# Lightning attention into a PReLU MLP: the opening's list laid out anew from finer statements

## The chip, the cores and the metric

The kernel runs on one core of one Trainium2 chip. The metric is device time in microseconds, from the first to the last instruction of an execution. The kernel before takes 214.34 us, the median of three runs (214.21 to 216.0).

## The reference

Two layers in a row. The first is a causal linear attention with decay ("lightning attention"): 4 batches, 8 heads, 768 positions, head size 64, in blocks of 64 positions with a running 64x64 state per head. The second is an MLP with a learned slope for negative values: 3072 tokens of 512 features to 2048 and back to 512.

```
for b in range(nb):                       # blocks of 64 positions
    intra = einsum('bhic,bhjc->bhij', qb, kb) * Dmask          # Dmask[i,j] = lam**(i-j), i >= j
    intra = einsum('bhij,bhjd->bhid', intra, vb)
    inter = einsum('bhid,bhde->bhie', qb * lam**(pos+1), kv_state)
    out[:, :, sl] = intra + inter
    kv_state = lam**block * kv_state + einsum('bhsd,bhse->bhde', kb * lam**(block-1-pos), vb)
h = x @ w_in                              # x: the attention's output, [3072, 512]
g = maximum(h, 0) + alpha * minimum(h, 0)
return g @ w_out
```

Inputs and output are float32; the kernel computes in float16 with float32 accumulation.

## The kernel before, in words

**Work.** The kernel takes blocks of 128 positions. The tokens are cut into six chunks c of 512 (256 positions of two batches). Chunks 0 and 1 are the first 256 positions of all four batches, chunks 2 and 3 the next, 4 and 5 the last. A chunk has four *units* (chunk, one of two batches, one of two groups of four heads), numbered 0 to 23; a unit covers two blocks. Units of chunks 0 and 1 have no state to read in their first block.

**A unit's steps.** `load` brings q, k or v of one batch (512 KB; 256 KB for one head group) on SP's DMA queue. `cast` makes float16 copies; `key_decayed` makes kdec, the keys times their decay. `transposes` (or `transposed`, q or k alone) turns q and k on TensorE through PSUM, with a copy to qkT; with engine "D" SP does it by a DMA. `decayed` makes qdT, the queries times their decay. `cluster(old, new)` then interleaves two units on TensorE: the carried part of the old unit (qdT against the states RD), the scores of the new one, the old one's output from its masked scores, and the new one's keys against values (the new state's increment). Behind these it records the mask products of the new unit (`sm`, two on VectorE), the copy of the old unit's output into the chunk's xT, and the new unit's state updates (R, by ScalarE and VectorE, and RD). So all of a cluster's statements stand in one piece in each engine's queue.

**A chunk's MLP.** `up(c, f)` is one of 16 tiles of hidden features: four 128x512 matmuls against w_in, then ScalarE makes m = relu(-h) and VectorE g = m*(1-alpha)+h (`slope_product`; with `later` it is recorded further down). `down(c, t, part, 4)` is a quarter of an output tile of 128 tokens, four matmuls against one quarter of w_out. So a chunk has 16 up-projections and 16 down parts of four matmuls each. `store` copies the result to SBUF and sends it.

**PSUM.** Eight banks: "acc" (two banks, one buffer, for a cluster's output and key-value products), s0 and s1 (scores), "op", "tk" and two buffers of "h" (up-projections, down tiles, transposes, fills). `fill` issues matmuls whose result nobody reads, to keep TensorE running.

**Order.** Nothing is scheduled by a compiler: each engine's queue holds its instructions in the order in which the statements are called. The program has three parts: a prefix (constants, decay tables), a long list of calls written out (L595 to L905: units 0 to 18, chunk 0's and 1's MLP and chunk 2's up-projections), and a loop over chunks 3 to 5 that weaves `up(c)`, `down(c-1)` and the steps of the next units. The list is what the change replaces.

**Weights.** w_in and w_out come in quarters of 512 hidden features (1 MB of float32 each, converted to float16 by the DMA, 512 KB as written), issued by GpSimd (`load_win`, `load_wout`), whose queue is in order: an issue waits for the casts and products listed ahead of it. `gate(i, which)` is a tiny DMA on SP's queue that reads one element of a quarter; since SP's queue is in order too, no later load is issued until that quarter has landed. In the list of before, SP meets `gate(1, "in")` right behind the load of q of (1,0).

```
    for gi in range(NHP):                      # up: w_in quarter f // 4
        nc.tensor.matmul(h_ps, lhsT=w_in_sb[:, gi, ts(f, 128)], rhs=x, start=(gi == 0), stop=(gi == 3))
    for f in range(part * n, part * n + n):    # down: w_out quarter `part`
        nc.tensor.matmul(o_ps, lhsT=lhs(c, f, t), rhs=w_out_sb[:, f, :], start=(f == 0), stop=(f == NF - 1))
```

Of the kernel before, what the change touches and what calls it, by code (L numbers as in the profile page):

```python
# [11 lines left out]
def kernel(  # L12
# [16 lines left out]
    nc = tc.nc  # L29
# [7 lines left out]
    B, H, S, D = q.shape  # L37
    assert (B, H, S, D) == (4, 8, 768, 64)
    L = 128
    W = 2 * L  # L40
    NC = (S // W) * 2
# [28 lines left out]
        for n in range(1, S // L)  # L70
# [24 lines left out]
    def load_win(i):  # L95
        nc.gpsimd.dma_start(  # L96
            out=w_in_sb[:, :, ts(i, 512)],
            in_=moe_w_in[:, ts(i, 512)].rearrange("(g p) f -> p g f", p=128),
        )

    def load_wout(i):
        nc.gpsimd.dma_start(
            out=w_out_sb[:, ts(i, 4), :],
            in_=moe_w_out[ts(i, 512), :].rearrange("(f p) d -> p f d", p=128),
        )
# [73 lines left out]
    )  # L179
    rev_f = const.tile([128, 2], fp32, name="rev_f")  # L180
# [29 lines left out]
    def decay_mask(hp):  # L210
        nc.scalar.activation(dmask[:, :, hp], dmask[:, :, hp], AF.Exp)

# [29 lines left out]
    T = {}  # L242
# [107 lines left out]
    def cluster(old, new, eng="A", state_first=False, own=False):  # L350

        acc = ps.tile([128, 2, 512], fp32, tag="acc", name="acc")
        ot = [acc[:, a, 0:256].rearrange("p (h i) -> p h i", h=2) for a in range(2)]
        kv = [acc[:, a, 256:384].rearrange("p (h d) -> p h d", h=2) for a in range(2)]
        if own:
            kv = [bank_of("h", "kv")[:, 0:128].rearrange("p (h d) -> p h d", h=2) for a in range(2)]
        if old is not None:
            co, bo, ho = units[old]  # L360
            pbo, bb = co // 2, 2 * (co % 2) + bo
            to = T[old]
            for a in range(2):
                if 2 * pbo + a == 0:
                    continue
                for hp in range(2):
                    nc.tensor.matmul(  # L367
                        ot[a][:, hp, :].rearrange("p (e j) -> p e j", e=2),
                        lhsT=RD[bb, ho][:, a, hp].rearrange("p h d -> p (h d)"),
                        rhs=to["qdT"][:, :, hp, ds(a * 64, 64)],  # L370
                        start=(hp == 0),
                        stop=False,
                        skip_group_check=True,
                    )
        if new is not None:
            c, bi, hh = units[new]
            pb, b = c // 2, 2 * (c % 2) + bi
            t = T[new]
            s = [ps.tile([128, 2, 2, L], fp32, tag=f"s{hl}", name=f"s{hl}") for hl in range(2)]
            for hp in range(2):  # L380
                for e in range(2):
                    for a, hl in QUADS:
                        p = ds(hl * 64, 64)
                        nc.tensor.matmul(  # L384
                            s[hl][ds(a * 64, 64), hp, 1 - e, :].rearrange("p (e j) -> p e j", e=2),
                            lhsT=t["qkT"][p, 1, e, hp, ds(a * 64, 64)],
                            rhs=t["qkT"][p, 0, :, hp, ds(a * 64, 64)],
                            start=True,
                            stop=True,
                        )  # L390
        if old is not None:
            for hp in range(2):
                for e in range(2):
                    for hl, a in QUADS:
                        p = ds(a * 64, 64)
                        nc.tensor.matmul(  # L396
                            ot[a][ds(hl * 64, 64), hp, :],
# [39 lines left out]
        def state():  # L437
# [18 lines left out]
            for a in range(2):  # L456
                if pb == 0:
                    continue
# [489 lines left out]
```

## Time and profile before

| what | value |
|---|---|
| median of three runs | 214.34 us |
| profiled execution, span | 215.6 us |
| TensorE busy | 206.4 us (96%) |
| VectorE, ScalarE, GpSimd busy | 131.6, 116.7, 86.8 us |
| DMA packets | 33.90 MB, mean 157 GB/s |
| read from HBM, written | 27.27 MB, 6.29 MB |

The profile is of one execution, and the times in it are counted from that execution's first instruction. A row of a timeline gives start, length, engine, source line, operation, what is written and read, shapes, count and, in brackets, how long the engine had sat idle and what ended that. A row of a group gives count, then busy time and the mean length of one instruction in ns, then idle time ahead of them and its cause. A chain row gives start, length and what the chain of waits passes through. Matmuls are pipelined, so the length of one is longer than the distance to the next. Line numbers are those of the kernel before.

### The profile page before, as it was taken

How to read it: one execution, taken by the hardware profiler on the slowest of the kernel's cores; microseconds unless marked ns; L12 is line 12 of the kernel's file. 1: busy time of each engine (PE TensorE's matmuls, PEld its weight loads, DVE VectorE, ACT ScalarE, POOL GpSimd, SP SyncE). 2: the span in 40 equal slices, each digit the busy share in tenths (PEclk: the TensorE clock that was granted, in tenths of full speed). 3: DMA queues.
4: the chain of work that ended last, by engine and by line, in shares of the span. 5: the costliest groups of instructions: out<-in, count | busy, mean ns of one | idle time of the engine just before them, and what ended most of it. 6: DMA issues, size and time to landing. Idle time of an engine off the chain costs nothing.

```text
span 215.6 us, 5212 instructions
## 1 busy us (share of the span) xinstructions
PE 206.4 (96%) x2089; PEld 107.3 (50%) x2089; DVE 131.6 (61%) x254; ACT 116.7 (54%) x220; POOL 86.8 (40%) x160
## 2 busy tenths in 40 slices
PE   7998997889999999999999999999999999999993
PEld 7564443445444545455554554554545444444453
DVE  7894887664298969879876645745646344444000
ACT  6996787335776544657855545544434534444121
POOL 7285254503592745577677366357311000000000
PEclk9999999999999999999999999999999999999999
DMA  5999999999999999699549997043011011110212
GB/s 164 295 270 206 244 237 249 160 248 281 240 284 144 294 237 271 161 255 173 71 128 227 249 238 203 13 100 97 2 52 49 14 38 49 50 49 3 97 49 97
DMA packets 62478, 33.90 MB, mean 157 GB/s; under 512 B 18150, under 2 KB 59510, under 8 KB 62454
## 3 DMA queue, kind: packets, MB, share of 16 engines
q1 hardware_dynamic: 58182, 29.37, 56.6%
q0 software_dynamic: 4224, 4.19, 12.1%
q8 instruction: 16, 0.26, 0.5%
q14 instruction: 8, 0.07, 0.1%
q10 hardware_dynamic: 48, 0.01, 0.0%
HBM read 27.27 MB, written 6.29 MB: 156 GB/s over the span
## 4 chain that ended last, share of the span: by engine, by line
PE 72%; DMA 20%; SPq 3%; POOL 2%; ACT 1%; issue 1%; DVE 0%; ACTq 0%
PE o_ps L518 30%; PE h_ps L479 29%; PE o_ps L547 6%; DMA vraw<-in_v_dram 5%; DMA kraw<-in_k_dram 5%; DMA w_in_sb<-in_moe_w_in_dram 5%; DMA w_out_sb<-in_moe_w_out_dram 5%; PE s L384 2%; PE acc L396 2%; SPq L87 2%; PE acc L367 2%; PE acc L411 1%; POOL qk L252 1%; ACT o_sb L531 0%; POOL w_in_sb L96 0%
## 5 line engine op out<-in xcount | busy, mean ns | idle before, releaser
L503 DVE SCALAR_TENSOR_TENSOR g<-m,oma,h_ps 128x512 f16<-128x512 f32 x96 | 70.5, 745 | 55.7 <-ACT m L487 54.2
L479 PE MATMUL h_ps<-xT,w_in_sb 128*128 128x512 f16 x384 | 93.4, 379 | 0.6 <-DMA w_in_sb<-in_moe_w_in_dram 0.4
L487 ACT ACTIVATE m<-h_ps 128x512 f32<-128x512 f32 x96 | 56.9, 597 | 50.6 <-PE h_ps L479 49.0
L518 PE MATMUL o_ps<-w_out_sb,g 128*128 128x512 f16 x320 | 79.5, 379 | 2.3 <-DMA w_out_sb<-in_moe_w_out_dram 2.3
L479 PEld LDWEIGHTS <-w_in_sb 128*128 128x128 f16 x384 | 36.5, 98 | 43.5 <-DMA w_in_sb<-in_moe_w_in_dram 0.6
L518 PEld LDWEIGHTS <-g 128*128 128x128 f16 x320 | 30.3, 98 | 38.1 <-DMA w_out_sb<-in_moe_w_out_dram 1.8
L461 POOL COPY RD<-R 64x128 f16<-64x128 f16 x64 | 19.6, 306 | 41.0 <-DVE R L447 39.3
L422 DVE TENSOR_TENSOR sm<-s,dmask 128x512 f16<-128x512 f32 x48 | 30.8, 683 | 7.3 <-PE s L384 7.0
L340 POOL TENSOR_TENSOR qdT<-qkT,qdecay 128x512 f16<-128x512 f16 (+1 forms) x19 | 20.1, 1059 | 11.8 <-ACT qkT L248 6.0
L531 ACT ACTIVATE o_sb<-o_ps 128x512 f32<-128x512 f32 (+2 forms) x26 | 14.7, 564 | 17.8 <-PE o_ps L547 10.9
L248 ACT ACTIVATE xT<-acc 128x512 f16<-128x512 f32 x21 | 12.5, 597 | 12.1 <-PE acc L411 8.1
L278 POOL TENSOR_TENSOR kdec<-kraw,kdecay 128x512 f16<-128x512 f32 x16 | 17.2, 1075 | 3.0 <-DMA kraw<-in_k_dram 3.0
L547 PE MATMUL o_ps<-w_out_sb,g 128*128 128x512 f16 (+2 forms) x96 | 14.1, 308 | 0.0
L447 DVE SCALAR_TENSOR_TENSOR R<-R,rdecay,acc 128x64 f16<-128x64 f16 x56 | 12.3, 272 | 1.2 <-ACT R L444 1.2
L252 POOL CAST qk<-kraw 128x512 f16<-128x512 f32 x12 | 7.4, 613 | 14.1 <-ACT RD L443 9.7
L547 PEld LDWEIGHTS <-g 128*128 128x128 f16 x96 | 8.1, 98 | 6.1
L252 POOL CAST v<-vraw 128x512 f16<-128x512 f32 x13 | 8.2, 628 | 5.3 <-DMA vraw<-in_v_dram 5.2
L396 PE MATMUL acc<-sm,v 64*64 64x128 f16 x384 | 10.0, 217 | 0.2 <-issue 0.2
L384 PE MATMUL s<-qkT 64*64 64x128 f16 x384 | 10.0, 222 | 0.0
L367 PEld LDWEIGHTS <-RD 128*128 128x128 f16 x80 | 6.4, 98 | 5.8 <-ACT RD L443 0.7
L252 POOL CAST qk<-qraw 128x512 f16<-128x512 f32 x13 | 8.0, 616 | 2.2 <-DMA qraw<-in_q_dram 2.0
L367 PE MATMUL acc<-qdT,RD 128*128 128x128 f16 x80 | 8.4, 219 | 0.0
(67 smaller groups left out, 124.2 us busy)
## 6 DMA issues: line engine op xcount, KB each, us to landing
out_dram<-o_sb SPq DMA_DIRECT2D x23, 256.0 KB, 2.5
qraw<-in_q_dram SPq DMA_DIRECT2D x10, 512.0 KB, 5.6
kraw<-in_k_dram SPq DMA_DIRECT2D x10, 512.0 KB, 7.9
vraw<-in_v_dram SPq DMA_DIRECT2D x10, 512.0 KB, 6.0
w_in_sb<-in_moe_w_in_dram POOLq DMA_DIRECT2D x4, 512.0 KB, 9.4
w_out_sb<-in_moe_w_out_dram POOLq DMA_DIRECT2D x4, 512.0 KB, 9.9
kraw<-in_k_dram SPq DMA_DIRECT2D x4, 256.0 KB, 4.3
qraw<-in_q_dram SPq DMA_DIRECT2D x4, 256.0 KB, 4.5
```

What stands on the lines that cost most here:

```text
L252: nc.gpsimd.tensor_copy(out=out, in_=in_)
L278: engine(eng).tensor_tensor(out=kdec, in0=kr, in1=kdecay[:, ds(4 * hh, 4), :].rearrange("p h e -> p e h").unsqueeze(3).to_broadcast([128, ...
L340: engine(eng).tensor_tensor(out=qdT[:, :, :, p], in0=(t["qps"] if eng == "P" else t["qkT"][:, 0])[:, :, :, p], in1=qdecay[:, hh, :, :, p], ...
L367: nc.tensor.matmul(ot[a][:, hp, :].rearrange("p (e j) -> p e j", e=2), lhsT=RD[bb, ho][:, a, hp].rearrange("p h d -> p (h d)"), rhs=to["qd ...
L422: nc.vector.tensor_tensor(out=sm, in0=s[hl], in1=mask_of(hl, hh), op=ALU.mult)
L461: nc.gpsimd.tensor_copy(out=RD[b, hh][p, a, :, hl, :], in_=R[b, hh, 2 * pb + a][p])
L479: nc.tensor.matmul(h_ps[:, 0:n] if bi is None else h_ps[:, 0:n].rearrange("p (e j) -> p e j", e=2), lhsT=w_in_sb[:, gi, ts(f, 128)], rhs=x ...
L487: nc.scalar.activation(m[:, 0:n], h_ps[:, 0:n], AF.Relu, scale=-1.0)
L503: nc.vector.scalar_tensor_tensor(out=g, in0=mv, scalar=oma[:, f : f + 1], in1=hv, op0=ALU.mult, op1=ALU.add)
L518: nc.tensor.matmul(o_ps, lhsT=lhs(c, f, t), rhs=w_out_sb[:, f, :], start=(f == 0), stop=(f == NF - 1),)
L531: nc.scalar.activation(o_sb[:, 0:n], o_ps[:, 0:n], AF.Copy)
L547: nc.tensor.matmul(o_ps[:, 0:n], lhsT=lhs(c, f, t), rhs=w_out_sb[:, f, ds(x, n)], start=(f == 0), stop=(f == NF - 1),)
```

## The change

1. The cluster is taken apart into statements of its own: `carry`, `scores`, `outs`, `keys` (TensorE), `masked` (the mask products, one or both), `output` and `state`, whose engines can be chosen for each call. `pecluster` is the TensorE part alone. `scores` and `keys` can take their PSUM banks by name, so that several units of the opening are in flight. `cluster` remains for the loop.
2. `mask_direct(hp)` makes a head pair's decay mask by two Exp on ScalarE and one product with a 0/1 mask `keep`; it serves head pairs 2 and 3. Pairs 0 and 1 keep the old way.
3. `load_win` and `load_wout` take first tile and count. w_in's first quarter comes in two pieces of two tiles; w_out's first two quarters are issued right behind w_in's last.
4. The list is laid out anew, to the end of chunk 2's up-projections: another order of loads (keys of unit 2 first), other engines for casts, copies and state, slope products apart from their up-projections throughout. The opening has 17 fills of 128x512 in place of 23. SP meets its first gate, on w_out's second quarter, behind nine full loads (those of chunk 1 and three of chunk 2); `gate(1, "in")` and `gate(3, "in")` stand further down. The first up-projection is that of tile 2, in bank "tk", behind all four units' outputs.

```diff
-    def load_win(i):
+    def load_win(f, n):
         nc.gpsimd.dma_start(
-            out=w_in_sb[:, :, ts(i, 512)],
-            in_=moe_w_in[:, ts(i, 512)].rearrange("(g p) f -> p g f", p=128),
+            out=w_in_sb[:, :, ds(f * 128, n * 128)],
+            in_=moe_w_in[:, ds(f * 128, n * 128)].rearrange("(g p) f -> p g f", p=128),
         )
+    def mask_direct(hp, eng="G"):
+        for hl in range(2):
+            h = 2 * hp + hl
+            nc.scalar.activation(dmask[:, hl, hp], rel_f, AF.Exp, scale=loglam[:, h : h + 1])
+        engine(eng).tensor_tensor(out=dmask[:, :, hp], in0=dmask[:, :, hp], in1=keep.unsqueeze(1).to_broadcast([128, 2, 3, 64]), op=ALU.mult)
+    def pecluster(old, new, own=False):
+        if old is not None:
+            carry(old)
+        if new is not None:
+            scores(new)
+        if old is not None:
+            outs(old)
+        if new is not None:
+            if old is None and not own:
+                ACC[new, "own"] = ps.tile([128, 2, 512], fp32, tag="acc", name="acc")
+            keys(new, None if own else (new, "own") if old is None else old)
...
+    load(0, 1, "k", 0)
+    query_decay(0, 1)
+    fill(4, "h", None, 512)
+    mask_logs(1)
+    load(0, 0, "q", 0)
+    load(0, 0, "k", 0)
+    key_decay()
+    mask_logs(0)
+    mask_direct(2, "V")
+    cast(0, "q16", "A")
+    load(0, 1, "q", 0)
...
+    key_decayed(0, "G")
+    cast(2, "q16", "G")
+    cast(0, "k16", "G")
+    transposes(0, "V", False)
+    transposed(2, 0, "V", "h")
+    decayed(2, "G")
+    mask_direct(3, "V")
+    load_win(0, 2)
+    scores(0, ("s0", "s1"))
+    masked(0, 0)
+    load_win(2, 2)
...
+    output(2, "A")
+    cast(1, "v16", "G")
+    masked(1, 0)
+    load(1, 0, "k", None)
+    load_win(12, 4)
+    state(3, "V", "G")
+    decayed(3, "G")
+    keys(1, None, ("op", "tk"))
+    scores(3, ("s0", "s1"))
+    masked(3, 1)
+    masked(3, 0)
+    state(1, "V", "A")
+    carry(1)
+    load_wout(0, 4)
+    outs(1)
+    output(1, "A")
+    load_wout(4, 4)
+    load(1, 0, "v", None)
+    carry(3)
+    outs(3)
+    output(3, "A")
+    up(0, 2, None, "tk", True)
...
+    pecluster(None, 4, False)
+    cast(6, "k16", "A")
+    cast(7, "k16", "G")
+    state(4, "V", "V")
+    transposes(5, "A", False)
+    load(2, 0, "k", None)
+    gate(1, "out")
+    down(0, 0, 0, 4, "h", True)
+    down(0, 0, 1, 4, "h", True)
+    load_wout(8, 4)
```

More of the change, by code (lines that the diff above doesn't have):

```diff
@@ L348 @@
     QUADS = [(x, y) for x in range(2) for y in range(2)]
[L350 to L372, printed above, removed]
+    ACC = {}
@@ new lines @@
+    key_decayed(3, "V")
+    cast(3, "q16", "G")
+    carry(0)
+    key_decayed(1, "G")
+    cast(1, "q16", "A")
+    load(1, 0, "q", None)
+    transposes(1, "V", False)
+    scores(2, ("h", "h"))
+    masked(2, 1)
+    query_decay(2, 1)
+    outs(0)
+    cast(2, "v16", "A")
+    keys(2, None, ("s0", "s1"))
+    state(2, "A", "A")
+    load_win(8, 4)
+    query_decay(3, 0)
+    fill(4, "tk", None, 128)
+    output(0, "V")
+    transposes(3, "A", False)
+    query_decay(0, 0)
+    masked(2, 0)
```

847 lines of the change are left out of this document (468 added, 379 removed).

## Prediction

> **What bounds the kernel now.** I read the page's first lines, then busy time by stage, then TensorE's waits and the chain that ended last.
>
> ```profile
> span 215.6 us, 5212 instructions
> 0.00:19.68 19.68, 16.99 (x290) 11.49 (x290) 16.18 (x45) 16.22 (x39) 13.38 (x30) 1.00 1.02 237
> 19.68:35.00 15.32, 15.32 (x112) 7.51 (x112) 11.94 (x18) 11.89 (x23) 4.77 (x6) 1.00 1.17 243
> 35.00:50.00 15.00, 12.05 (x203) 6.84 (x203) 9.52 (x21) 5.61 (x14) 5.57 (x8) 1.00 1.07 215
> 50.00:215.60 165.60, 162.07 (x1488) 81.43 (x1485) 93.91 (x172) 82.98 (x147) 63.09 (x116) 1.00 0.57 135
> 19.68 4.49 PE L479 MATMUL h_ps<-xT,w_in_sb 128*128 128x512 f16 x20 [0.43 <-DMA w_in_sb<-in_moe_w_in_dram]
> PE o_ps L518 <- DMA w_out_sb<-in_moe_w_out_dram: 2.3, 3, 1.3
> PE h_ps L479 <- DVE g L503: 0.2, 1, 0.2
> ```
>
> After each stage's length stand the busy times of PE, weight loads, DVE, ACT and POOL, then clock, DMA share and GB/s. The first up-projection starts at 19.68, when the first quarter of w_in has landed. From there TensorE does only useful work: full to 35, short of 2.95 us between 35 and 50 (the three waits for w_out are most of it), and short of 0.2 in the long rest, apart from the tail behind the last matmul. So the time is the start of the up-projections, plus 3.17 us (2.95 + 0.22) of holes, plus a constant: 215.6 - 19.68 - 3.17 = 192.75. The change leaves the useful matmuls alone; its six dropped 128x512 fills stand before the first up-projection. It can move the start and the holes, nothing else. Which wait ends last, the chain says:
>
> ```profile
> 23.98 11.28 DMA kraw<-in_k_dram
> 35.31 0.62 POOL qk L252
> 36.67 9.89 DMA w_out_sb<-in_moe_w_out_dram
> 46.59 1.89 PE o_ps L518 x8
> ```
>
> The key load of unit pair 6/7 lands at 35.3; GpSimd, whose queue is in order, casts it, and only then issues w_out's later quarters; the third lands at 46.6 and TensorE goes on. This link (key load, cast, w_out issue) is also in the new list.
>
> **The start of the up-projections.** Both lists take the twelve half loads of units 0 to 3 first, and both must finish four units. Before, the end of this stage is w_in; I work out who ends it now.
>
> ```profile
> 6.12 0.62 POOL L252 CAST qk<-kraw 128x512 f16<-128x512 f32 x1 [0.80 <-DMA kraw<-in_k_dram]
> L278 POOL TENSOR_TENSOR kdec<-kraw,kdecay 128x512 f16<-128x512 f32 x4 | 4.2, 1050 | 1.8 <-DMA kraw<-in_k_dram 1.8
> 32.22 0.61 PE L306 MATMUL tp<-ident,qk 128*128 128x128 f16 x8
> 32.76 0.42 PE L384 MATMUL s<-qkT 64*64 64x128 f16 x16
> L422 DVE TENSOR_TENSOR sm<-s,dmask 128x512 f16<-128x512 f32 x8 | 5.1, 684 | 0.8 <-PE s L384 0.6 <-issue 0.2
> L278 DVE TENSOR_TENSOR kdec<-kraw,kdecay 128x512 f16<-128x512 f32 x3 | 2.0, 682 | 0.0
> L447 DVE SCALAR_TENSOR_TENSOR R<-R,rdecay,kv 128x64 f16<-128x64 f16 x8 | 1.9, 275 | 0.5 <-ACT R L444 0.5
> L250 DVE COPY qkT<-tp 128x1024 f16<-128x1024 f16 x1 | 0.7, 683 | 0.0
> L250 DVE COPY qkT<-tpx 128x512 f16<-128x512 f16 x1 | 0.4, 414 | 0.0
> L250 DVE CAST xT<-acc 128x512 f16<-128x512 f32 x1 | 0.7, 680 | 0.0
> L250 DVE CAST v<-vraw 128x512 f16<-128x512 f32 x1 | 0.4, 418 | 0.0
> L340 DVE TENSOR_TENSOR qdT<-qkT,qdecay 128x256 f16<-128x256 f16 x4 | 1.6, 420 | 0.0
> L444 ACT ACTIVATE R<-kv 128x128 f16<-128x128 f32 x4 | 1.1, 278 | 0.1
> 15.23 1.28 DVE L422 TENSOR_TENSOR sm<-s,dmask 128x512 f16<-128x512 f32 x2
> ```
>
> The third load lands at 6.1. It now holds unit 0's keys, and GpSimd takes kdec (1.05) and two casts (0.62 each) from there: 8.4. Eight transposes (0.54 to the next start) end at 9.0. VectorE copies qkT (0.68) and unit 2's half (0.41), multiplies a mask (new; between 0.41 and 0.68 by its size, I take 0.5) and makes the slopes: 10.6 with overlaps. Then its queue to the last mask product of unit 3 holds 8 mask products (5.47), 6 state updates (1.65), a value cast, a qdT (0.42 each), a kdec, a qkT, an xT copy (0.68 each) and one 128x128 state copy (ACT's 0.28 stands for it): 10.3 for 20. Neighbours overlap by 2 x 0.684 - 1.28 = 0.09, which takes off 1.7. Waits come to about 1.2, most of it for unit 2's state, which ACT writes (two half copies and the 0.28) behind TensorE's keys. That is 20.4. Unit 1's state copy and updates (0.28 + 0.47) follow, and they free the PSUM bank "tk" that the first up-projection writes: **start 21.2, 1.5 later than before.** ACT's four output copies and TensorE's eight score and output groups run beside this chain. Bounds: 20.3 if the waits vanish, 22.4 if each of the four cross-engine handovers costs 0.3 more.
>
> Of the rest of the opening: the pieces of w_in's first quarter are issued behind unit 2's qdT at about 10.7, about when the whole quarter was before (10.5 in the next rows; it landed by 19.7), and are there by 19 to 20; with the start at 21.2 they are covered, and the split earns nothing. The two masks by direct Exp spare VectorE four products and give it two; both stand ahead of 10.6 and behind the load, so nothing. The dropped fills: nothing, the clock column reads 1.00 in every stage.
>
> **The holes behind it.** The gates are the main edit here.
>
> ```profile
> 10.51 0.93 POOL L96 DMA_DIRECT2D w_in_sb<-in_moe_w_in_dram  x1
> 9.82 0.83 SPq L87 DMA_DIRECT2D qraw<-in_q_dram  x1
> 22.16 0.73 SPq L113
> 14.00:15.00 1.00, 1.00 (x53) 0.86 (x50) 0.76 (x3) 1.00 (x3) 0.64 (x2) 1.00 1.20 269
> 3.00:14.00 11.00, 10.41 (x149) 6.99 (x149) 9.73 (x25) 10.13 (x26) 6.82 (x14) 1.00 1.11 288
> 16.00:24.00 8.00, 7.36 (x93) 3.60 (x92) 4.82 (x11) 5.43 (x13) 3.17 (x5) 1.00 1.24 206
> q0 software_dynamic: 422, 0.43, 75.0%
> q1 hardware_dynamic: 592, 0.30, 39.3%
> DMA to landing us min/median/max: 6.4/9.9/11.3
> 109.42 0.86 PE h_ps L479 x4
> 108.55 0.86 PE o_ps L518 x4
> 44.01 0.28 PE L367 MATMUL acc<-qdT,RD 128*128 128x128 f16 x2
> 44.91 1.04 PE L518 MATMUL o_ps<-w_out_sb,g 128*128 128x512 f16 x4
> ```
>
> SP's gate on w_in's second quarter (L113) held every load behind q of (1,0) from 10.7 to 22.2. It now stands far down, and the first gate SP meets, on w_out's second quarter, comes after nine full loads, three of them for units 8 to 11. These now share the DMA engines with w_in and w_out.
>
> Alone, q/k/v move at 288 GB/s (1.82 us for a full load), weights at 206 (2.55 us for a quarter; bytes as written). The queue rows are for 29.5 to 33 us, where both wait: weights 0.43 MB in 3.5 us (4.3 us a quarter), the others 0.30 MB (6.1 us a load). From about 14, when the slower weights set in (the rate falls from 288 to 269), six quarters (w_in and half of w_out, now issued without a break) take 25.8 us, to 39.8, and four loads 24.4, to 38.4; with 1 to 2 us for the slowest engine, that of units 6/7's keys lands at about 39.7, against 35.3 before. Of the six, w_in's second lands at 22.6 and is asked for at 24.7, and the last lands at 39.8 (or an engine's 1 to 2 us later) and is asked for at 39.5; what is lost there, the next link swallows. GpSimd casts the keys (0.62) and issues w_out's third quarter at 40.3. From issue to landing w_out took 6.4 to 11.3, at the median 9.9, and these are the ends. It is alone on its queue here, which speaks for the lower one, with five loads on the other, which speaks for the median: I take 8.7. **Landing 49.0**, between 46.7 and 51.6.
>
> When does TensorE ask for it? Behind the start stand 16 up-projections and 8 down parts of 0.86 (20.6), the transposes of four units (0.54 each) and three clusters (0.9, 0.9 and, without an old unit, 0.5): 25.1 us, so 46.3. The work left then is 192.75 - 25.1 = 167.65.
>
> By hand: 49.0 + 167.65 = 216.65, that is +1.05 on the profiled 215.6. The old 3.17 us of holes are gone, replaced by +1.5 of start and 2.7 of new holes. The profiled execution is 1.3 above the median of the runs, 214.34; I lay the difference on the median: 215.4. Later relays (split groups, casts moved among the engines) are put at nothing: the stages past 50 had 0.2 us of holes, with VectorE at 57% (93.91 of 165.6); without that cover a late mask product costs up to 0.68 each.
>
> [...]
>
> **The rivals.** *Faster:* the third quarter lands before 46.3, and the start alone decides: 21.2 + 192.75 = 213.95, or 213.05 with a start at 20.3; on the median 212.7 and 211.8. For it: w_out's first half now follows w_in without a break, and the 6.4. Against: the key load that GpSimd must cast first has six quarters beside it. *Slower:* the ungated loads take the engines from the weights. With 11.3 from issue to landing the third quarter is there at 51.6, and 51.6 + 167.65 = 219.25, +3.65: 218.0. It passes +1% when that quarter lands after 50.1. For it: the median of 9.9, which alone gives 50.2; against: the gate still stops SP after nine loads. *Not as it says:* the start stays at 19.7, where it was; TensorE then only waits longer at the third quarter, and the time is my forecast's, in whose chance it lies.
>
> **How the numbers follow.** About 1% (2.1 us) is what a measurement of this kernel can tell from no change. Forecast, within 1%: 0.46. Slower rival: 0.38. Faster by over 1% (start near 20.3 and no hole): 0.16. The range reaches from a start at 20.8 without a hole (213.55, -2.05: 212.3) to the slower rival's 218.0.
>
> **What would show it.** First up-projection at 21.2, released by VectorE and not by DMA; the key load of units 6/7 landing near 39.7; a TensorE wait of 1 to 3 us for w_out's third quarter near 46 to 49; no wait for its first. I am wrong if the up-projections start before 20.3, if no such wait is seen, or if holes of over a microsecond stand behind 55.

## The result, and the profile after

The changed kernel takes 223.55 us, the median of four runs (223.08 to 225.37), against 214.56 for the kernel before (214.21 to 216.0): a ratio of 1.041, with an interval of 1.034 to 1.047. It is slower by 4%, where the forecast was within 1%, and it lies above the range.

The page of the changed kernel, first line, then busy time by stage (the columns as before: length; PE, weight loads, DVE, ACT, POOL; clock, DMA share, GB/s):

```profile
span 221.9 us, 5196 instructions
0.00:19.68 19.68, 14.03 (x148) 8.79 (x149) 13.76 (x33) 11.09 (x27) 13.20 (x28) 0.83 1.04 245
19.68:26.88 7.20, 4.86 (x140) 3.37 (x139) 5.49 (x14) 4.13 (x10) 4.28 (x8) 1.00 1.20 216
26.88:35.00 8.12, 8.12 (x38) 3.72 (x38) 5.55 (x8) 5.77 (x11) 1.19 (x2) 1.00 1.20 216
35.00:50.00 15.00, 14.54 (x166) 7.87 (x164) 13.13 (x24) 8.58 (x17) 5.00 (x7) 1.00 1.17 265
80.00:110.00 30.00, 28.43 (x403) 14.80 (x400) 26.61 (x59) 15.34 (x27) 20.41 (x39) 1.00 0.95 202
```

Three things differ from before. TensorE is busy for 14.03 of the first 19.68 us, where it was 16.99, and its clock there reads 0.83 in place of 1.00. The up-projections begin at 26.1. And 1.57 us are idle between 80 and 110, where the kernel before had none; in return the 2.95 us of holes between 35 and 50 have shrunk to 0.46. The opening in slices of 2.5 us, from the same view, and below it what TensorE waited for and what the other two engines did (start, length, engine, operation, and in brackets the idle time ahead and what ended it):

```profile
7.50:10.00 2.50, 0.83 (x9) 0.66 (x10) 0.42 (x1) 2.50 (x9) 2.01 (x3) 0.89 1.16 292
10.00:12.50 2.50, 2.50 (x18) 1.35 (x20) 1.49 (x3) 0.49 (x1) 0.69 (x1) 0.50 1.16 291
12.50:15.00 2.50, 1.90 (x37) 0.97 (x36) 2.01 (x4) 0.54 (x2) 2.50 (x5) 0.92 1.15 289
17.50:20.00 2.50, 2.50 (x64) 2.24 (x63) 1.77 (x3) 0.82 (x4) 1.93 (x4) 0.56 1.34 209
```

```profile
9.57 1.03 PE L320 MATMUL tp<-ident,qk 128*128 128x128 f16 x8 [1.49 <-POOL qk L266]
16.67 0.37 PE L378 MATMUL acc<-qdT,RD 128*128 128x128 f16 x2 [2.27 <-DVE qdT L354]
25.56 0.27 PE L378 MATMUL acc<-qdT,RD 128*128 128x128 f16 x2 [0.79 <-ACT xT L262]
26.11 0.60 PE L539 MATMUL h_ps<-xT,w_in_sb 128*128 128x512 f16 x2
26.88 1.46 PE L539 MATMUL h_ps<-xT,w_in_sb 128*128 128x512 f16 x6 [0.16 <-ACT xT L262]
6.86 1.55 POOL L292 TENSOR_TENSOR kdec<-kraw,kdecay 128x512 f16<-128x512 f32 x1 [2.77 <-DMA kraw<-in_k_dram]
14.28 0.62 POOL L266 CAST qk<-kraw 128x512 f16<-128x512 f32 x1
14.37 1.50 DVE L264 CAST v<-vraw 128x512 f16<-128x512 f32 x1
15.79 0.82 DVE L354 TENSOR_TENSOR qdT<-qkT,qdecay 128x256 f16<-128x256 f16 x1
```

TensorE does 0.83 us of work between 7.5 and 10, and then the clock reads 0.50: eight transposes take 1.03 us where before they took 0.61. VectorE's value cast takes 1.50 us beside a cast and a w_in issue on GpSimd (14.28 to 15.58), in place of the 0.42 the prediction used. The last carry (25.56) and the first up-projection's later matmuls (26.88) each stand behind an output copy on ScalarE. Two matmuls start at 26.11 and the rest at 26.88, so that the start counts as 26.45: two of 0.22 each are done by 26.88.

By the prediction's formula the parts add up: 26.45 + 192.75 + 2.3 of holes (0.46 between 35 and 50, 0.26 between 50 and 80, 1.57 between 80 and 110) is 221.5, against a span of 221.9.

### The profile page after: what moved, and what is told of

It reads as the page before. It is cut to its first block, busy times and chain, and to the rows that moved or that the text cites. A ratio compares the mean times of both kernels' runs of the same rounds, so it can differ in the third digit from the quotient of the medians.

```text
span 221.9 us, 5196 instructions
## 1 busy us (share of the span) xinstructions
PE 208.3 (94%) x2083; PEld 107.8 (49%) x2083; DVE 141.7 (64%) x272; ACT 111.1 (50%) x207; POOL 85.5 (39%) x157
## 4 chain that ended last, share of the span: by engine, by line
PE 74%; DVE 7%; DMA 5%; POOL 4%; issue 4%; ACT 2%; SPq 1%; POOLq 0%; ACTq 0%; DVEq 0%
PE h_ps L539 32%; PE o_ps L578 25%; PE o_ps L607 6%; DMA vraw<-in_v_dram 3%; PE s L396 3%; PE acc L420 3%; DVE sm L408 2%; DMA kraw<-in_k_dram 2%; PE acc L378 2%; POOL RD L495 1%; DVE R L481 1%; PE tp L320 1%; DVE g L563 1%; POOL kdec L292 1%; ACT xT L262 1%
## 5 line engine op out<-in xcount | busy, mean ns | idle before, releaser
L495 POOL COPY RD<-R 64x128 f16<-64x128 f16 x64 | 19.7, 308 | 44.0 <-DVE R L481 42.2
L408 DVE TENSOR_TENSOR sm<-s,dmask 128x512 f16<-128x512 f32 x48 | 31.5, 682 | 1.5 <-PE s L396 1.4
L354 POOL TENSOR_TENSOR qdT<-qkT,qdecay 128x512 f16<-128x512 f16 (+1 forms) x18 | 18.6, 1034 | 20.7 <-ACT qkT L262 14.2
L591 ACT ACTIVATE o_sb<-o_ps 128x512 f32<-128x512 f32 (+2 forms) x26 | 14.7, 564 | 21.7 <-PE o_ps L607 10.9
L292 POOL TENSOR_TENSOR kdec<-kraw,kdecay 128x512 f16<-128x512 f32 x18 | 20.0, 1116 | 3.6 <-DMA kraw<-in_k_dram 3.6
L262 ACT ACTIVATE xT<-acc 128x512 f16<-128x512 f32 x19 | 11.3, 596 | 14.1 <-PE acc L444 9.5
L262 ACT ACTIVATE qk<-qraw 128x512 f16<-128x512 f32 x17 | 10.6, 624 | 1.4 <-DMA qraw<-in_q_dram 1.3
L396 PEld LDWEIGHTS <-qkT 64*64 64x64 f16 x384 | 6.5, 110 | 2.9 <-issue 1.0
```

The lines of the kernel that those rows point to most:

```text
L262: nc.scalar.activation(out, in_, AF.Copy)
L292: engine(eng).tensor_tensor(out=kdec, in0=kr, in1=kdecay[:, ds(4 * hh, 4), :].rearrange("p h e -> p e h").unsqueeze(3).to_broadcast([128, ...
L354: engine(eng).tensor_tensor(out=qdT[:, :, :, p], in0=(t["qps"] if eng == "P" else t["qkT"][:, 0])[:, :, :, p], in1=qdecay[:, hh, :, :, p], ...
L396: nc.tensor.matmul(S[x][hl][ds(a * 64, 64), hp, 1 - e, :].rearrange("p (e j) -> p e j", e=2), lhsT=t["qkT"][p, 1, e, hp, ds(a * 64, 64)], ...
L408: nc.vector.tensor_tensor(out=sm, in0=S[x][y], in1=mask_of(y, units[x][2]), op=ALU.mult)
L495: nc.gpsimd.tensor_copy(out=RD[b, hh][p, a, :, hl, :], in_=R[b, hh, 2 * pb + a][p])
```

## The experiments

The theories. **A**: the loss is made in the new opening alone. **B**: the lists behind it, or the loads that no longer wait, lose too. **C**: idle stretches put TensorE's clock at half, and that carries the loss of the opening. **D**: VectorE and GpSimd slow each other, so that durations taken from before are too short. Kernels of one group ran on the same chip, beside the kernel before; "span" is that of the profiled execution; a run's time is some 1.8 us longer than its span. The "opening" is the list up to the first up-projection, the "rest" what follows to the end of the written-out list. A ratio has its interval in brackets.

### Old and new halves

`e1_old_opening`: the old opening, and the new rest.

```
-    fill(2, "h", None, 512)
...
-    output(3, "A")
+    query_decay(1, 1)
...
+    gate(1, "in")
...
+    cluster(3, None, "A")
+    load_wout(0, 4)
+    load_wout(4, 4)
+    load(1, 0, "v", None)
     up(0, 2, None, "tk", True)
```

> The list of before up to the first up-projection (its loads, gate, clusters and casts), with w_out's first two quarters and the load of v of (1,0) put behind it, and from the first up-projection on the list of after. Theory A (the new opening alone is the loss, by a late start of the up-projections): start near 19.7, holes behind it 2 to 4 us, span 214.5 to 216.5, ratio to before 0.995 to 1.005. Theory B (the new list behind the opening is the loss, or the ungated loads are): start 19.7, but holes of 8 us and more, ratio 1.03 or more.

Ratio 1.036 [1.028, 1.043], span 223.3. TensorE's row where it goes wrong:

```profile
36.11 1.87 PE L539 MATMUL h_ps<-xT,w_in_sb 128*128 128x512 f16 x4 [4.40 <-DVE g L563]
```

The start is back at 19.74, and the time is hardly better. The wait that I had kept holds the keys of batch pair (1, 0) back, and the new list asks for them earlier: VectorE's in-order queue stands at their cast, the gated products behind it keep the PSUM banks, and TensorE idles for 4.40 us. So this run mixes two lists that don't fit; e5 separates them.

`e2_new_opening`: the new opening, and the old rest.

```
     output(3, "A")
-    up(0, 2, None, "tk", True)
...
+    up(0, 3, None, "h")
...
```

The old rest's own loads of w_out's first two quarters and of v of (1,0) are left out, since the new opening has them.

> The list of after up to the first up-projection, and from there the list of before (its second and third load of w_out's first half and of v of (1,0) left out, since the opening has them). Theory A: start near 26.4, holes below 1 us, span 219.5 to 220.5, ratio 1.02 to 1.04. Theory B: ratio below 1.01.

Ratio 1.012 [1.004, 1.020], span 218.1: the least slow of the mixtures with the new opening. Between 80 and 110 TensorE is busy for 30.00 of 30 us. Its opening is the same list as the changed kernel's and goes another way: the clock is full up to 19.68, VectorE reaches the value cast 1.6 us earlier, before GpSimd's, and it takes 0.43. TensorE's rows of this opening, and the first up-projections:

```profile
7.68 0.40 PE L340 MATMUL tpx<-ident,qk 128*128 128x128 f16 x4 [1.49 <-ACT qk L262]
9.43 0.62 PE L320 MATMUL tp<-ident,qk 128*128 128x128 f16 x8 [1.35 <-POOL qk L266]
23.57 6.73 PE L539 MATMUL h_ps<-xT,w_in_sb 128*128 128x512 f16 x20
```

The first two gaps are together longer than the changed kernel's 0.64 and 1.49 us, yet here the clock holds over them, and with no fill added the start is 23.57, 2.9 us earlier than 26.45. So it is the clock, more than the gaps' own length, that makes the opening late. The half clock comes later, under the first up-projections (0.67 between 19.68 and 30): their first twenty matmuls take 6.73 us, where the kernel before's took 4.49.

### The opening's gaps and casts

`e3_fills` (two more fills, behind the first copies and behind the first keys) and `e4_vcast_on_act` (the slow value cast on ScalarE):

```
     transposed(2, 1, "V", "h")
+    fill(6, "h", None, 512)
...
     keys(0, None, ("h", "h"))
+    fill(8, "tk", None, 512)
```
```
-    cast(3, "v16", "V")
...
     cast(0, "v16", "A")
+    cast(3, "v16", "A")
```

> After, with 6 more fills of 128x512 behind the first half transpose of unit 2 and 8 behind unit 0's key products, where TensorE stands idle. Theory C (the clock granted to TensorE falls to half in these idle stretches, and transposes, scores and key products at half clock carry the chain): granted clock 0.95 or more up to 20 us, start 1.5 to 2.5 earlier than 26.4. Theory D (VectorE and GpSimd slow each other; the half clock is beside the chain): start within 0.5 of 26.4.

> After, with unit 3's value cast on ScalarE (idle from 10.5 to 14.4) and not on VectorE, where it took 1.50 us against 0.42 before. Theory D: the qdT of unit 0 ends 1 to 1.7 us earlier than 16.6, start 1 to 1.7 earlier than 26.4. Theory C: start at most 0.5 earlier.

Spans 220.8 and 221.5, single runs of 222.53 and 223.26 us. Fills brought the clock to 1.00 up to 19.68 and the start to 23.67, behind a 0.90 us wait for w_in, but then the clock was at 0.83 up to 30, and the first ten matmuls of the up-projections took 3.66 us in place of 2.2. With the cast moved, the start came at 24.66, 1.8 us earlier and by more than theory C allowed, but here the clock also stayed full between 13.4 and 23.6, so the run doesn't part the two theories; the first up-projections were again at half clock. Each mends its place; the lost clock moves on.

`e6_fills_all`: fills in all five idle stretches, those of e3 and three more.

```
     scores(3, ("s0", "s1"))
+    fill(3, "h", None, 512)
...
     outs(1)
+    fill(4, "h", None, 512)
...
     outs(3)
+    fill(4, "h", None, 512)
```

> The changed kernel with fills in all five idle stretches of its opening. Theory C (half clock behind idle stretches carries the loss of the opening): granted clock 1.00 from 0 to 35, up-projections from 23 to 23.7 and at 0.22 us each from the first on; against e3_fills, whose first ten took 3.66 us in place of 2.2, that is 1.5 us less: span 219.3, ratio about 1.02. If the clock doesn't matter, the start and the span stay at e3_fills' 23.67 and 220.8, or get worse by the fills' own 4.1 us of TensorE time. Theory D (VectorE and GpSimd slow each other): start no earlier than 23, whatever the clock.

Ratio 1.029 [1.024, 1.034], span 219.5, by stage and at the start:

```profile
0.00:19.68 19.68, 17.54 (x245) 10.24 (x245) 16.18 (x39) 13.24 (x32) 14.57 (x29) 1.00 1.05 246
19.68:25.00 5.32, 5.13 (x69) 2.62 (x70) 2.67 (x9) 2.08 (x6) 3.01 (x6) 1.00 1.21 217
80.00:110.00 30.00, 28.40 (x405) 14.89 (x403) 26.36 (x57) 15.13 (x27) 20.93 (x39) 1.00 0.93 200
12.78 0.44 DVE L264 CAST v<-vraw 128x512 f16<-128x512 f32 x1
23.73 0.81 PE L539 MATMUL h_ps<-xT,w_in_sb 128*128 128x512 f16 x3
```

The clock holds, the value cast is back at 0.44 since it no longer meets GpSimd's, and the start moves from 26.45 to 23.73. Theory C's number (219.3) is met: 2.4 us of the span are the idle stretches and what they bring about. A start of 23.73 is still 2.5 later than I had it, and the waits between 80 and 110 are all still there.

`e8_fills_old_rest`: e2's edit and e6's together, this opening with the old rest.

> The new opening with fills in its five idle stretches, and the old list behind it. Theory C: against e2_new_opening (218.1, of which 2.3 us are its first twenty up-projections at half clock, 6.73 us in place of 4.4) the span falls to about 215.8, ratio 1.00 to 1.005. If the late chain of VectorE and GpSimd alone sets the start (theory D), it stays above 217. If A and B are both right, it is below e6_fills_all by the 1.7 us of waits that the new list has between 80 and 110.

Ratio 1.020 [1.014, 1.025], span 218.3: no better than e2, against theory C's 215.8. At full clock the up-projections caught up with w_in and waited for it 0.54 and 0.89 us, near 30.8 and 34.4. So 1.4 of the 2.2 us that the half clock had cost e2's first up-projections were waited for here.

`e9_kdec_apart`: e6 with VectorE's kdec of unit 2 behind the first qkT copy.

```
-    key_decayed(2, "V")
...
     transposed(2, 1, "V", "h")
+    key_decayed(2, "V")
```

> e6_fills_all with one line moved: VectorE's kdec of unit 2 behind its first qkT copy, where GpSimd's kdec and casts of unit 0 are over or nearly so. Theory D (VectorE and GpSimd slow each other): in e6_fills_all VectorE's kdec took 1.54 beside GpSimd's, in place of 0.68, and GpSimd's kdec and two casts 1.37, 1.07 and 0.61 in place of 1.05, 0.62 and 0.62. Apart, GpSimd is done at 8.5 to 8.7 in place of 9.39, the first mask product of unit 0 stands near 10.8 in place of 11.58, and the first up-projection near 23.0 in place of 23.73; span 218.8. If they don't slow each other, the first mask product stays at 11.5 or, with the kdec now in front of the qkT copies, gets later by up to 0.4, and the span stays at 219.5 or rises.

Ratio 1.029 [1.027, 1.031], span 219.5. First mask product 11.36 in place of 11.58, start 23.48. GpSimd's row says why it is less than a microsecond:

```profile
6.36 1.44 POOL L292 TENSOR_TENSOR kdec<-kraw,kdecay 128x512 f16<-128x512 f32 x1 [2.27 <-ACT dmask L219]
7.75 0.61 POOL L266 CAST qk<-qraw 128x512 f16<-128x512 f32 x1
```

GpSimd's two casts are back at 0.61, but its kdec still took 1.44, beginning while VectorE's mask product ran (6.34 to 6.90); and the transposes behind now waited for the six fills. The 0.7 us that I had expected of the start came to 0.25.

### The weights alone

`e7_weights_only`: the kernel before, w_in's first quarter in two pieces and w_out's first two quarters right behind w_in.

```
-    load_win(0)
+    load_win_piece(0, 2)
+    load_win_piece(2, 2)
...
     load_win(3)
+    load_wout(0)
+    load_wout(1)
...
-    load_wout(0)
...
-    load_wout(1)
```

> The kernel before with the two weight edits alone: w_in's first quarter in two pieces, w_out's first two quarters right behind w_in's last. By the prediction's steps: the 0.43 us wait ahead of the first up-projection stays or falls to 0 (start 19.3 to 19.7), the wait of 1.33 us for w_out's first quarter at 36.5 goes, and the keys of units 6 and 7, which now share the engines with two more quarters, land later than 35.3, so that the third quarter is awaited longer than before's 0.65. Sum between -1.5 and +2 us, ratio 0.993 to 1.01. If weights in this order were what cost the 9 us, the ratio would be 1.03.

`e10_weights_free`: the same without SP's wait.

```
-    gate(1, "in")
```

> e7_weights_only without the wait on w_in's second quarter that SP met before the keys of batch pair (1, 0): all of the change's edits to the loads' order around the weights, on the old lists. Without the wait the keys are issued near 10.7 in place of 22.84 and the 3.74 us hole of e7_weights_only at 34.8 goes; they share the engines with w_in, whose first quarter then lands near 20.6 as in e5_old_opening_free (start 20.6, 0.9 later than before); w_out's first quarter is there when asked for, the third quarter is issued behind the key load of units 6 and 7 near 39.5 and lands near 48, against TensorE's demand near 46.5. Sum 20.6 + 192.75 + 2 = 215.4 in the profiled execution, ratio 1.00 to 1.01. If the weights' order and not the opening were the loss, it would be 1.03.

Ratios 1.022 [1.016, 1.027] and 1.020 [1.013, 1.027]; spans 218.0 and 216.4. TensorE's rows, of e7 (the first) and of e10:

```profile
34.83 0.39 PE L332 MATMUL tpx<-ident,qk 128*128 128x128 f16 x2 [3.74 <-ACT qk L254]
```
```profile
20.47 3.63 PE L485 MATMUL h_ps<-xT,w_in_sb 128*128 128x512 f16 x16 [0.66 <-ACT xT L254]
24.42 1.04 PE L485 MATMUL h_ps<-xT,w_in_sb 128*128 128x512 f16 x4 [0.32 <-DMA w_in_sb<-in_moe_w_in_dram]
28.05 2.76 PE L485 MATMUL h_ps<-xT,w_in_sb 128*128 128x512 f16 x12 [0.64 <-ACT m L493]
31.75 1.90 PE L485 MATMUL h_ps<-xT,w_in_sb 128*128 128x512 f16 x8 [0.94 <-DMA w_in_sb<-in_moe_w_in_dram]
```

The weights' order on the old lists loses 2% either way, without the new opening, so theory A falls. With the wait kept, unit 4's keys come late (3.74 us, with the clock at half for 3.4 us behind it). Without it, w_in itself is late: TensorE catches up with it twice, and the start is 0.8 later, when w_in's second piece and the last output copy, which the row names, are both there at about 20.4. The longest wait of e10 is 1.34 us at 41.2, for a value cast that GpSimd reaches only behind the keys of units 6 and 7 (38.5) and two issues of w_out. In neither is there a wait for w_out's first three quarters; the waits have only changed their place.

`e5_old_opening_free`: e1 without that wait, the line `gate(1, "in")`.

> The old opening without the wait on w_in's second quarter that SP met there, and behind it the whole new list. Theory A (the loss is made in the opening alone): first up-projection at 19.7 to 20, holes behind it no more than before's 3.2 us, time within 1% of before. Theory B (the new list behind loses too): the same start, but the waits of 1.5 us in all between 80 and 110 that the changed kernel and the first two runs with this list show are there again, with further ones between 30 and 50; span some 215.6 + 0 to 3, ratio 1.00 to 1.015. The 4.40 us hole of e1_old_opening goes in both, if the held key load made it; if it stays, the list itself puts the key cast too early.

Ratio 1.028 [1.022, 1.034], span 220.6; e1's hole is gone. The start is 20.62, behind a 1.11 us wait for w_in, and the waits between 80 and 110 come to 1.92 us: theory B. A further hole of 2.00 us stands at 43.2, and these rows end it:

```profile
40.59 0.63 POOL L266 CAST v<-vraw 128x512 f16<-128x512 f32 x1
40.96 2.19 DVE L264 CAST qk<-qraw 128x512 f16<-128x512 f32 x1 [0.56 <-DMA qraw<-in_q_dram]
41.17 0.68 POOL L354 TENSOR_TENSOR qdT<-qkT,qdecay 128x256 f16<-128x256 f16 x1
41.80 1.05 POOL L292 TENSOR_TENSOR kdec<-kraw,kdecay 128x512 f16<-128x512 f32 x1
43.20 0.40 PE L320 MATMUL tp<-ident,qk 128*128 128x128 f16 x4 [2.00 <-DVE qk L264]
```

GpSimd runs without a break from 40.59 to 42.85, and VectorE's cast, of the kind that takes 0.42, ends at 43.15.

`e15_cast_apart`: e5 with that cast on ScalarE.

```
-    cast(6, "q16", "V")
+    cast(6, "q16", "A")
```

> e5_old_opening_free with one cast, of unit 6's queries, on ScalarE in place of VectorE. Theory D: on VectorE it took 2.19 us (0.42 is its time elsewhere) while GpSimd ran a cast, a query product and a key product beside it without a break, and TensorE waited 2.00 us for it at 43.2. On ScalarE, behind another cast, it ends near 42.2 in place of 43.1: the hole falls to 1.0 or less, and the clock of 0.89 between 35 and 50 rises; span 220.6 - 1 to - 2.5. If the load and not the cast is late, the hole stays at 2.0.

Span 220.3, a single run of 222.41 us. The cast was the cause: the hole falls to 1.00 and the clock between 35 and 50 returns from 0.89 to 1.00. But the gain is 0.3 us, though this run's start was also earlier (19.89, with the same opening list): TensorE, earlier by then, waits 1.50 us at 48.6 for w_out's third quarter, which e5 did not, and the waits between 80 and 110 grow from 1.92 to 3.05.

`e11_wout_quarter` and `e14_wout_order`: can the kernel before get rid of its own w_out waits? The first diff is against the kernel before, the second against e11.

```
-    gate(1, "in")
+    gate(0, "in")
...
     load_win(3)
+    load_wout(0)
...
-    load_wout(0)
```
```
-    transposed(4, 1, "A", "tk")
     up(0, 13, None, "h")
     up(0, 15, None, "h")
+    transposed(4, 1, "A", "tk")
     transposes(5, "A", False)
-    cluster(None, 4)
     up(0, 9, None, "op", True)
+    cluster(None, 4)
```

> The kernel before with w_out's first quarter alone issued behind w_in's last, and SP's wait put on w_in's first quarter in place of the second. The keys of (1, 0) are then issued near 20.4 in place of 22.9, w_in's start stays at 19.7, w_out's first quarter lands near 31 and its 1.33 us wait at 36.5 goes; the later waits for w_out of 0.33 and 0.65 stay or grow by up to 1. Time between -1.3 and +0.5 us of before, ratio 0.994 to 1.003. If the keys land later than in the kernel before, since four pieces of weights now run beside them, a wait for the transposes near 31 takes its place: ratio 1.005 to 1.01.

> e11_wout_quarter, whose one hole (2.03 us at 31.99, TensorE waiting for the cast of unit 4's keys) put the clock at half behind it, with two up-projections and, further on, one more taken ahead of the work that waits: they fill some 1.7 us of the hole. Then the clock holds and none of the kernel before's waits for w_out is left: span 215.3 - 1.7 - 1.3 (the first eight behind the hole took 2.89 in place of 1.73, the transposes 1.06 in place of 0.61) = 212.3, ratio 0.993 to 0.998. If the weights' order can't be improved since the engines are full either way, the wait shows up at the next load and the ratio is 1.00 or above.

Ratios 1.008 [1.005, 1.011] and 1.015 [1.008, 1.022]. e11's w_out waits are gone and a 2.03 us wait for unit 4's keys stands at 32.0; in e14 the filled hole came back as 2.16 us at 33.5, for a gated product whose relu stands behind the cast of these keys in ScalarE's queue. Neither beats the kernel before.

### Fills and copies

`e12_before_less_fills`: the kernel before without the six fills between its units.

```
-    fill(5, "h")
...
-    fill(5, "op")
...
-    fill(4, "tk")
...
-    fill(2, "tk")
...
-    fill(4, "tk")
...
-    fill(3, "op")
```

> The kernel before without its six fills (23 matmuls of 128x512) between the units of the opening; no useful work is left out. Theory C: its idle stretches then come to 1 to 1.5 us each, the granted clock falls below 1.00 between 8 and 20, the matmuls there take up to twice as long, and the first up-projection comes 0.5 to 2 us later than 19.7, or the first ones run at 0.43 each. If w_in's landing at 19.6 alone sets the start and the clock holds, nothing changes (span 215.6): then dropped fills cost nothing, as the prediction had it.

Span 214.7, a single run of 216.47 us (the kernel before beside it: 215.03 in the median). By stage, and the start:

```profile
7.50:10.00 2.50, 1.14 (x12) 0.75 (x10) 2.22 (x6) 2.50 (x6) 0.00 (x0) 0.52 1.16 291
10.00:20.00 10.00, 7.78 (x201) 6.09 (x200) 7.57 (x18) 8.00 (x24) 8.40 (x12) 0.50 1.22 247
20.00:25.00 5.00, 5.00 (x28) 2.08 (x28) 1.24 (x5) 1.96 (x4) 0.05 (x1) 0.53 1.18 188
35.00:50.00 15.00, 15.00 (x255) 8.53 (x254) 12.88 (x27) 8.88 (x22) 4.24 (x7) 1.00 1.18 245
20.73 1.89 PE L479 MATMUL h_ps<-xT,w_in_sb 128*128 128x512 f16 x4
```

The clock is at half from 7.6 to 24.7, the start is a microsecond later, and the first matmuls of the up-projections take about twice their 0.22. Yet the span isn't longer than the 215.6 of the profiled execution before: the holes between 35 and 50 are gone, since TensorE came later and found w_out there. Against the ordinary runs beside it (spans of 213.0 to 213.5, and one of 215.5) this single run is 1.2 to 1.7 us longer, so it doesn't show that the dropped fills were free.

`e13_lean`: e9 with fills no longer than the gaps (the first is shown; 8, 3, 4 and 4 become 4, 1, 3 and 3), and the state copies of line 495 on ScalarE.

```
-    fill(6, "h", None, 512)
+    fill(4, "h", None, 512)
...
-                nc.gpsimd.tensor_copy(out=RD[b, hh][p, a, :, hl, :], in_=R[b, hh, 2 * pb + a][p])
+                copy_on("A", RD[b, hh][p, a, :, hl, :], R[b, hh, 2 * pb + a][p])
```

> e9_kdec_apart with its fills cut to the length of the gaps (4, 4, 1, 3 and 3 matmuls in place of 6, 8, 3, 4 and 4), and, far behind, the state copies that feed the carry of units 8 to 15 on ScalarE in place of GpSimd. Opening: if the fills' overhang is what remains of the late start, first up-projection at 22.2 to 22.6 in place of 23.48, the clock still at 1.00; if VectorE's chain or ScalarE's output copies end last anyway, 23.2 or later. Between 80 and 110: if GpSimd's queue makes the waits there (casts and key products ahead of these copies), the 0.6 us wait for GpSimd and with it most of the 1.9 us of idle time goes, to under 1; if it is VectorE, at 88% there, it stays at 1.5 or more. Both: span 217.5, ratio 1.018 to 1.022.

Ratio 1.074 [1.066, 1.081], span 230.6. The second edit was a mistake: the waits for GpSimd's copies are gone, and in the waits' view TensorE now waits for ScalarE, above all for the output copies queued behind them:

```profile
PE o_ps L578 <- ACT o_sb L591: 6.6, 7, 1.6
```

The opening tells what it was for:

```profile
21.37 0.82 PE L141 MATMUL unread<-ident 128*128 128x512 f16 x3
22.90 0.82 PE L539 MATMUL h_ps<-xT,w_in_sb 128*128 128x512 f16 x3 [0.72 <-DMA w_in_sb<-in_moe_w_in_dram]
```

The attention work and its fills end at 22.2, and the first up-projection then waits for w_in.

`e16_lean_order`: this opening, the copies on GpSimd again, and one key product behind them.

```
-    key_decayed(12, "G")
...
     state(11, "A", "A")
+    key_decayed(12, "G")
```

> The opening of e13_lean, the state copies of units 8 to 15 on GpSimd again, and GpSimd's key product of unit 12 behind the state copies of unit 11 in place of ahead of them. Opening as in e13_lean: first up-projection at 22.9, released by the landing of w_in's second piece. Near 85 to 88, where the carry of unit 11 waits for these copies (0.34 and 0.64 in the changed kernel): the copies start about 1.0 earlier, by the key product's 1.05, and the two waits fall to 0.3 or less in all. Span 22.9 + 192.75 + 1.6 + about 0.4, as this sum fell short of e6_fills_all: 217.6; ratio 1.018 to 1.022. If GpSimd's queue isn't the cause, the two waits stay and the span is 218.4.

Ratio 1.025 [1.021, 1.029], span 219.4. Start 22.57, released by w_in, and two shorter waits for it follow (0.26 and 0.14). The carry of unit 11 waits 0.65 in place of 0.34 and 0.64, but the displaced key product is then 0.27 late, and between 80 and 110 the idle time stays at 1.87. The order of these two is not the cause of these waits: the four copies alone take 2.04 us, and a cast that waits for its load stands ahead of them in both. Of the start's 1.2 us on e6 no more than 0.1 reached the end; w_in's waits and those between 80 and 110 account for some 0.7 of it, the rest I can't place.

## Why the prediction was wrong, step by step

**The constant and the form of the sum** held: start + holes + 192.75 gives 221.5 for a span of 221.9, so nothing else moved. It closes within a microsecond in e6, e8, e9, e10 and e16 too, and misses 1.5 us in e15 and 2.7 in e13. Where TensorE ran at half clock behind the start (e1 to e5, e7, e11, e12, e14) it falls 1.2 to 3.7 us short: the sum has no term for the clock.

**The start was the step that failed**: 21.2 predicted, 26.45 measured, which is the whole error of the sum (216.65 against 221.9). Three of its terms were mis-sized and add up to the 5.25 us (2.72, 1.38 and 1.15); a fourth was wrong and cost nothing here.

- *"The dropped fills: nothing, the clock column reads 1.00 in every stage."* The column read 1.00 because the fills were there: without six of them (e12) it reads 0.50 from 10 to 20. I counted fills and not the gaps they stood in. With every gap filled (e6) the start is 23.73, and with the same list at full clock (e2) 23.57: 2.7 us of the 5.25 come with the half clock, which the bare gaps let in. By the chain of waits of the changed kernel against e6's, unit 0's first mask product came at 13.16 in place of 11.58, at half clock; and that delay put the value cast beside GpSimd's, so that unit 0's qdT came at 15.79 in place of 13.14.
- *VectorE's and GpSimd's durations taken from before.* In e6 GpSimd was done with unit 0 at 9.39, not 8.4 (0.2 of it the load), and unit 3's kdec took 1.63 in place of 0.68. At the last mask product this has come to 1.4 us: 21.78 in place of 20.4. This is read from the rows; the one run that parts two of these instructions (e9) gained 0.25 us. The warning stood in the profile of before. Its group of these casts, with shortest, median and longest time in ns, is this row, and I took the 418:

```profile
L250 DVE CAST v<-vraw x2: 418/843/1268, 43.5 to 84.7; 128x512 f16<-128x512 f32 x2
```

- *"ACT's four output copies ... run beside this chain."* The last two don't. Unit 1's output copy frees the PSUM buffer that unit 3's carry needs, and unit 3's copy feeds the up-projection: from the last mask product to the start pass 1.95 us in e6, of which up to 0.3 are the last two fills' (0.15 each), in place of 0.8.
- *"The pieces ... are there by 19 to 20 ... covered."* They were issued at 12.6 and 13.5, not at 10.7, and landed at 19.7 and 22.2, by the trace's DMA records, and `up(0, 2)` reads the second piece first. It cost nothing in the changed kernel, which was later still, but w_in is what the start waits for in the leanest openings (22.57 and 22.90) and in e3 (23.67).

**The holes.** The third quarter of w_out landed at 47.8 (predicted 49.0), issued at 39.4 (40.3). That this agrees is luck, for the link behind it was another. GpSimd's rows:

```profile
38.21 0.67 POOL L354 TENSOR_TENSOR qdT<-qkT,qdecay 128x256 f16<-128x256 f16 x1 [10.15 <-ACT qkT L262]
38.83 0.61 POOL L266 CAST qk<-kraw 128x512 f16<-128x512 f32 x1
39.38 0.79 POOL L102 DMA_DIRECT2D w_out_sb<-in_moe_w_out_dram  x1
```

The keys of units 6 and 7, issued at 14.7, had landed 19.0 us later, at 33.7 (predicted 39.7). GpSimd stood for 10.15 us at unit 4's qdT, listed ahead of their cast, until ScalarE had copied unit 4's transposes, which came late with TensorE's late start. No wait for w_out came of it either, since TensorE asked at some 26.45 + 25.1 = 51.5, not at 46.3. So the 2.7 us of holes were, by luck, about the right size at the wrong place: 0.46 up to 50, 0.26 up to 80, and 1.57 between 80 and 110, where I had put *"later relays ... at nothing"*. There VectorE is busy for 26.61 of 30 us and GpSimd for 20.41, against 25.44 and 17.60 before. They occur with the new rest in every run, whatever the opening, and never with the old one. What exactly makes them stays open, after e13 and e16.

**The slower rival**, to which I gave 0.38, had the right sign by the wrong mechanism: the weights' order and the loads that no longer wait do cost 2% on the old lists (e10), but in w_in and in a late value cast, not in w_out's third quarter. The weights' order alone costs the same (e7), so what the loads add isn't shown. In the changed kernel TensorE never waits for w_in: the late opening hides it.

**The median.** I laid a difference of the profiled execution on the median of the runs, and took that execution for 1.3 us above the median. But 215.6 is a span and 214.34 a time, and the time is 1.7 to 1.9 us longer than the span in every listed run but one (2.1). So 215.6 stands for a time of some 217.4, 3 us above the median: of the 8.2 us between the forecast 215.4 and the measured 223.55, 5.25 are the start and 2.9 are this step. Span to span the change is +6.3 us, median to median +9.0. In the runs listed beside the experiments, the kernel before mostly has spans of 213 to 214.5, and start plus constant alone, without any hole, are 19.68 + 192.75 = 212.4. So a part of the 3.17 us of holes that I counted as gone was not there in an ordinary run. That is argued; no profile of such a run exists.

So the loss isn't one thing. On the old lists the weights' order with the freed loads costs 2.0% (e10); with the new rest it is 2.8% (e5); with the new opening at full clock no more (e6, 2.9%); and the half clock with what follows from it adds the last 1.2%, to 4.1%. Intervals of neighbours in this row overlap, the last pair's only just, at 1.034, and the parts don't add: the new opening with the old rest costs least of all (e2, 1.2%).

## What to carry to other kernels

A clock column of 1.00 says what the fills did, not that they are spare: before dropping or moving any, list the gaps between a new order's matmuls and see how much work is left among them (in the changed kernel 3.41 us with 1.38 and with 1.52 us of work were followed by a clock of 0.50, and 3.41 us with 2.08 by 1.00). Take a duration with its longest case and with what ran on GpSimd beside it, since one list can fall either way when its phase shifts (the value cast of one opening took 0.43 us in e2 and, reached 1.6 us later, 1.50 in the changed kernel). Where waits for transfers follow, a gain ahead of them can be swallowed (e8, e16), so ask of each saving what it would wait for next. And before laying a difference in span on a median of times, see that the profiled execution is an ordinary one.

## What was not expected of the hardware

*The clock.* In the changed kernel the clock reads 0.50 from 9.47, behind two idle stretches of 0.64 and 1.49 us with 0.4 us of work between them. In fine slices of the traces it is at half from 9.47 to 12.88 and from 16.30 to 19.71, each 3.41 us; in e2 from 21.32 to 28.14, twice that, and in e12 from 7.61 to 24.68, five times that. Divided at these edges into stretches of 3.41 us, the ten traces with such a dip (the changed kernel, e1 to e5, e7, e11, e12, e14) show, up to 56 us, that the clock fell behind stretches in which TensorE was busy for about 0.1 (e7) to 1.85 us (e3) and held behind those with 2.05 (e2) or more. It came back behind 2.73 (e3) to 3.41 us of work (e2, e12) and stayed at half behind 1.91 (e1) to 2.78 (e12), so for the return the busy time alone doesn't decide. The stretch ahead of the changed kernel's first fall, from 6.06 to 9.47, wasn't idle: it still had 1.38 us of work. And the fall comes at other places in runs of one list: e2, with the changed kernel's opening, kept 1.00 up to 21.32 and fell there, behind 1.70 us of work. What makes the 3.41 us isn't shown.

*VectorE beside GpSimd.* A cast from SBUF to SBUF took 0.42 us with GpSimd idle (43.47 in the kernel before), 1.27, 1.50 and 2.19 beside GpSimd (84.71 there, 14.37 in the changed kernel, 40.96 in e5), and in the longest case ended 0.30 us behind GpSimd's unbroken row of a cast and two products (to 42.85). So in e5 the end of the VectorE cast came behind that whole row of instructions following each other on GpSimd, not just behind the first of them, which ended at 41.22. Mask products, which read PSUM, kept their 0.67 to 0.68: 0.67 at 18.59 in the changed kernel beside a query product on GpSimd, 0.68 at 16.25 in e6 beside its kdec. Why the one kind got longer and the other didn't, no run shows.
